# Queries and keys of a softmax attention block projected by Strassen's method

## Chip, cores, metric

One core of a Trainium2 chip. The metric is the device time of one execution in microseconds (us); of several runs the median is given.

## The reference, cut to what matters

Two attention blocks read the same x (2048 tokens, 1024 features, 32 heads of 32) and are mixed by a gate. Block A is a linear attention, block B a softmax attention. All inputs are float32.

```python
x = A_x                                             # 2048 x 1024
g = sigmoid((x * gate_w).sum(-1, keepdims=True))
a = A_ref(x, A_wqkv, A_wo)                          # linear attention
b = B_ref(x, B_wqkv, B_wo)
out = g * a + (1 - g) * b

def B_ref(x, wqkv, wo):                             # wqkv: 1024 x 3072
    q, k, v = heads(x @ wqkv)
    p = softmax(q @ k.T * 32 ** -0.5)
    return heads_joined(p @ v) @ wo
```

The change is in `x @ wqkv` of block B: the columns of queries and keys (the first 2048).

## The kernel before

**Products of three.** An operand of a projection is split into a rounded upper part (`copy` on ACT, called hi) and the remainder (`tensor_sub`, lo); `split` does both. `three` issues three matmuls for each 128 rows of the contraction: hi by hi, hi by lo, lo by hi. One matmul has a 128x128 stationary and a 128x512 moving operand. The contraction of 1024 is `NK` = 8 such steps, so a 128x512 output takes 24 matmuls.

**Stages, in order.**
1. *Value chunk 0 of block B* (512 of 1024 columns). x transposed (`xT`) is loaded in 128x512 pieces, split, and stays in `big[0]` to `big[15]` (128x2048 tiles). The first 8 token tiles go through all 8 steps of the contraction together, in 8 banks, as x arrives; the other 8 follow tile by tile.
2. *Queries and keys of block B.* `order` runs over 8 groups `g` of 128 columns, 4 token chunks `j` of 512, and `sec` (0 queries, 1 keys): 64 units. The weights' columns are stationary, x is moving; a unit's output (4 heads by 512 tokens) is split by ACT and DVE and both parts are stored to `qk_d`. Beside it run two generators, one step per unit: `gate` (loads 128x512 of x into one buffer, and multiplies it by `gate_w` with a running sum on DVE in its next step) and `spill` (stores both parts of x, two transfers a unit, to `xs`, for the later projections of block A).
3. *Value chunk 1*, as the first 16 units of the generator `linear`; its stationary operand is the x that is still in SBUF (`xstat`). `load_head(0)` comes at its fifth unit, `load_head(1)` at its sixth. The score maxima of head 0 (`maxima`) are mixed into these units.
4. *The rest*: the heads of block B (`heads_`), the linear projections of block A from the spilled x (`load_half`, three buffers `xh_t`), the output.

Up to stage 2 the instructions of every engine stand in program order. From stage 3 on a planner chooses at each step which of the generators issues next, by modelled times `T` of the engines; on the chip, too, every engine runs its instructions in the order written. All loads and stores are issued by SyncE (SP) in that order, and SP waits for what a transfer needs before it issues it.

**Names that the change touches.** `xpart` (a resident piece of x), `want_x`, `want_w`, `want_g` and `pump` (loads of stages 1 and 2 with six raw buffers), `v_out` (a value tile's way out), `gate`, `spill`, `load_half`, `linear`. `bank[0]` to `bank[7]` are the eight PSUM banks. Line 157, 160 and 162 of the profile are the matmuls of `three`, 300 and 301 the two halves of `split`, 427 the gate's multiplication, 176 every DMA on SP, 853 to 867 the fills in `load_q` and `load_k`.

## Time and profile before

| | us |
|---|---|
| median of 3 runs | 2867.18 (2864.64 to 2867.98) |
| span of the profiled execution, first to last instruction | 2865.2 |
| TensorE busy | 2856.9 |
| ScalarE (ACT), VectorE (DVE), GpSimd (POOL) busy | 1525.8, 2037.4, 1909.1 |

The page gives no own time for the profiled execution beside its span; the median of the runs is 2.0 us above that span. DVE, ACT and POOL are the engines of the element-wise work; PE is TensorE, PEld its weight loads. A row such as `L301 DVE TENSOR_TENSOR mid<-bank,mid 128x512 ... x64 | 44.2, 691` is line 301 of the kernel, 64 instructions that read a bank and `mid` and write `mid`, busy for 44.2 us together and 691 ns each. Rows of a timeline begin with the start and the duration in us; what stands in brackets is the idle time before it and what ended that. Rows of the windows begin with a stretch of the span; they give its length, the busy time and number of instructions of each engine, the granted TensorE clock, the share of the 16 DMA engines that was busy, and GB/s.

### The profile page before, as it was taken

Reading aid. Unit: us, or ns where it says so; the run is one execution under the profiler, and the core shown is the slowest. Engines: PE = TensorE matmul, PEld = TensorE weight load, DVE = VectorE, ACT = ScalarE, POOL = GpSimd, SP = SyncE. Lnnn points to the kernel's source line nnn. Section 1 sums busy time; section 2 is a strip of 40 time slices with the busy share of each in tenths; the row PEclk is TensorE's granted clock in tenths of the full one; section 3 lists DMA queues with packets and bytes.
Section 4 is the critical chain, followed back from the end, with each engine's and each line's share of the span. In section 5 each row is a group of like instructions: output and inputs, shape, how many; then the busy total and the mean of one; then the engine's idle time right before and its main releaser. Section 6 shows DMA issues by size and latency. Waiting matters only on the chain.

```text
span 2865.2 us, 46266 instructions
## 1 busy us (share of the span) xinstructions
PE 2856.9 (100%) x16136; PEld 2089.8 (73%) x16136; DVE 2037.4 (71%) x3372; ACT 1525.8 (53%) x2866; POOL 1909.1 (67%) x894
## 2 busy tenths in 40 slices
PE   9999999999999999999999999999999999999999
PEld 8888888867766776677767777777676666676787
DVE  3232113888888888888888888788888887887522
ACT  4111111466676667666666666566666665666400
POOL 0000001299999999999999999889889888885000
PEclk9999999999999999999999999999999999999999
DMA  6687333333343434333434344455656554634542
GB/s 198 209 268 243 121 121 107 108 90 98 101 133 98 104 100 129 93 96 95 128 106 100 100 119 139 143 171 171 201 173 190 135 161 138 160 109 132 195 151 77
DMA packets 348292, 394.97 MB, mean 138 GB/s; under 512 B 103214, under 2 KB 192558, under 8 KB 348060
## 3 DMA queue, kind: packets, MB, share of 16 engines
q1 hardware_dynamic: 334460, 378.91, 43.6%
q0 software_dynamic: 13600, 13.11, 3.4%
q8 instruction: 128, 2.10, 0.3%
q14 instruction: 104, 0.85, 0.1%
HBM read 268.70 MB, written 108.79 MB: 132 GB/s over the span
## 4 chain that ended last, share of the span: by engine, by line
PE 99%; DMA 1%; ACT 0%; issue 0%; SPq 0%; POOL 0%; DVE 0%; ACTq 0%
PE bank L1076 17%; PE bank L157 16%; PE bank L160 16%; PE bank L902 16%; PE bank L162 16%; PE bank L1233 16%; PE bank L967 1%; PE bank L686 1%; PE bank L575 0%; PE bank L959 0%; DMA big<-wa 0%; DMA big<-in_a_wqkv 0%; PE bank L646 0%; ACT big L1079 0%; PE bank L919 0%; DMA extra<-in_b_wqkv 0%
## 5 line engine op out<-in xcount | busy, mean ns | idle before, releaser
L1168 POOL TENSOR_TENSOR big<-big,big 128x512 f32<-128x512 f32 (+2 forms) x694 | 1643.5, 2372 | 119.1 <-ACT big L1079 76.5
L907 DVE TENSOR_REDUCE mx<-bank 128x1 f32<-128x512 f32 x2048 | 1308.2, 681 | 297.0 <-PE bank L902 292.9
L1079 ACT ACTIVATE big<-bank 128x512 f32<-128x512 f32 x2048 | 1179.8, 601 | 432.9 <-PE bank L1076 361.0
L1076 PE MATMUL bank<-big,big 128*128 128x512 f32 x1888 | 742.4, 394 | 0.2 <-ACT big L1079 0.2
L902 PE MATMUL bank<-big,big 128*128 128x512 f32 x1888 | 739.7, 392 | 0.3 <-ACT big L1079 0.3
L157 PE MATMUL bank<-big,big 128*128 128x512 f32 x1704 | 665.2, 390 | 0.4 <-ACT big L300 0.4
L160 PE MATMUL bank<-big,big 128*128 128x512 f32 x1704 | 664.0, 390 | 0.0
L162 PE MATMUL bank<-big,big 128*128 128x512 f32 x1700 | 662.5, 390 | 0.0
L1233 PE MATMUL bank<-big,mid 128*32 128x512 f32 x4096 | 454.1, 593 | 0.0
L1076 PEld LDWEIGHTS bank<-big,big 128*128 128x128 f32 x1888 | 354.1, 188 | 125.6 <-issue 46.9
L902 PEld LDWEIGHTS bank<-big,big 128*128 128x128 f32 x1888 | 354.5, 188 | 75.1 <-ACT big L1079 2.9
L157 PEld LDWEIGHTS bank<-big,big 128*128 128x128 f32 x1704 | 320.0, 188 | 69.7 <-issue 0.8
L160 PEld LDWEIGHTS bank<-big,big 128*128 128x128 f32 x1704 | 320.0, 188 | 67.0 <-DVE big L301 0.2
L162 PEld LDWEIGHTS bank<-big,big 128*128 128x128 f32 x1700 | 319.2, 188 | 66.3
L1233 PEld LDWEIGHTS bank<-big,mid 128*32 128x32 f32 x4096 | 142.7, 110 | 265.1 <-issue 265.1
L853 POOL MEMSET big<- 32x512 f32 (+1 forms) x4 | 3.7, 949 | 458.2 <-PE bank L160 458.2
L1184 DVE TENSOR_TENSOR bank<-bank,big 128x512 f32<-128x512 f32 x364 | 251.2, 690 | 5.9 <-ACT big L1079 3.9
L301 DVE TENSOR_TENSOR mid<-bank,mid 128x512 fp32r<-128x512 f32 x64 | 44.2, 691 | 263.4 <-ACT mid L300 263.4
L300 ACT CAST mid<-bank 128x512 fp32r<-128x512 f32 x64 | 37.6, 587 | 291.6 <-PE bank L162 272.2
L1164 POOL TENSOR_TENSOR big<-big,big 128x1536 f32<-128x1536 f32 (+1 forms) x31 | 121.4, 3915 | 40.3 <-ACT big L1079 40.3
L157 PE MATMUL bank<-big,xh 128*128 128x512 f32 x344 | 135.2, 393 | 1.7 <-ACT big L1079 1.1
L160 PE MATMUL bank<-big,xh 128*128 128x512 f32 x344 | 134.8, 392 | 0.3 <-DMA big<-wa 0.3
(95 smaller groups left out, 1735.8 us busy)
## 6 DMA issues: line engine op xcount, KB each, us to landing
big<-xs SPq DMA_DIRECT2D x256, 256.0 KB
big<-qk SPq DMA_DIRECT2D x720, 64.0 KB
qk<-mid SPq DMA_DIRECT2D x128, 256.0 KB
xh<-xs SPq DMA_DIRECT2D x128, 256.0 KB
big<-oA SPq DMA_DIRECT2D x84, 256.0 KB
xs<-big SPq DMA_DIRECT2D x64, 256.0 KB
oA<-mid SPq DMA_DIRECT2D x64, 256.0 KB
big<-big POOLq DMA_DIRECT2D x50, 256.0 KB, 5.6
```

Source lines behind the costliest of these rows:

```text
L157: yield nc.tensor.matmul(ps, sh, mh_, start=(kt == 0), stop=False)
L160: yield nc.tensor.matmul(ps, sh, ml_, start=False, stop=(late and kt == NK - 1))
L162: yield nc.tensor.matmul(ps, sl, mh_, start=False, stop=(kt == NK - 1))
L301: eng.tensor_sub(lo, src, f32(hi))
L902: nc.tensor.matmul(bank[b], q[:, t % TPC * P:(t % TPC + 1) * P], k[:, j * C:(j + 1) * C], start=True, stop=True)
L907: nc.vector.tensor_reduce(m[:, t, j:j + 1], bank[b], AX.X, ALU.max)
L1076: nc.tensor.matmul(bank[b], k[:, t * P:(t + 1) * P], q_cols(h, j), start=True, stop=True)
L1079: nc.scalar.activation(pr_t[i][:, j * C:(j + 1) * C], bank[b], AF.Exp, scale=SCALE)
L1164: nc.gpsimd.tensor_add(lacc[:, :qp], pr(0)[:, :qp], pr(1)[:, :qp])
L1168: nc.gpsimd.tensor_add(lacc[:, sl], lacc[:, sl], pr(t)[:, sl])
L1184: nc.vector.tensor_add(lacc[:, qp:] if t == NT - 1 else l_b[:, :n], l_b[:, :n], src)
L1233: nc.tensor.matmul(av_b[j * DH:(j + 1) * DH, :], v[:, t, :], pr(t)[:, j * C:(j + 1) * C], start=(t == 0), stop=(t == NT - 1))
```

## The change

The tokens are taken in two halves `J` of 1024, the contraction as 4 pairs of steps (even `l = 0`, odd `l = 1`), and two column groups `g`, `g+1` of queries or keys are computed at a time by Strassen's method in Winograd's form: a *quad* has four outputs of 128x512 (two groups by two token chunks) from seven products of 4 steps (`KH`), 12 matmuls each.

- **Sides of x.** From the four raw pieces of a pair POOL makes T1 to T4 (`sides`), which ACT and POOL split (`split_sides`, `last_side`). X11, T1, T2, X21, T3, X22 and T4 are the moving operands of products 0 to 6. T4 takes the place of X12 once X12 was used by the value pass and spilled.
- **Weights.** Four 128x512 raw tiles per quad (`load_quad`, two quads ahead) are combined by DVE and split by ACT with DVE or POOL (`quad_weights`, during the quad before) into a ring of 14 slots. They are loaded and made once for each half of the tokens.
- **Sums.** `quad` issues the products into six banks in turn; DVE adds them up in `P1`, `U2`, `W2`, `C22`. Each output is split by ACT and POOL and stored in two transfers.
- **Beside a quad**, one step of each after every product: the next quad's weights, T4 (in the first quad of a half), a spill of x, and a step of the gate. The gate now takes 128x256 pieces (64 steps) in one buffer, `gate_x`. The eighth quad of a half has other company: `change` or `leave`.
- **Value chunk 0** is computed in each half before its quads (`v_pass`, 8 tiles at once). Its split weights are stored in the first half (`store_wv`) and loaded again for the second (`load_wv_again`).
- **Value chunk 1** no longer finds x in SBUF: `linear` takes it from `xs` by `load_half`, as the projections of block A do. `load_head(0)` comes at its first unit, `load_head(1)` at its second.

The core of the diff:

```diff
+    def sides(raws, i):
+        r11, r12, r21, r22 = raws
+        nc.gpsimd.tensor_sub(r11, r12, r11)
+        nc.gpsimd.tensor_sub(r12, r22, r12)
+        nc.gpsimd.tensor_sub(r22, r22, r11)
+        nc.gpsimd.tensor_sub(t4_raw[i], r21, r22)
...
+    def quad_weights(raws, J, f):
+        w11, w12, w21, w22 = raws
...
+        part(0, w11, nc.gpsimd)
+        part(6, w22, nc.vector)
+        nc.vector.tensor_add(w22, w21, w22)
+        nc.vector.tensor_sub(w21, w11, w21)
+        yield
+        part(1, w22, nc.gpsimd)
+        nc.vector.tensor_sub(w11, w22, w11)
+        yield
+        part(3, w12, nc.gpsimd)
+        part(2, w11, nc.vector)
+        yield
+        nc.vector.tensor_sub(w12, w12, w11)
+        part(4, w21, nc.gpsimd)
+        yield
+        part(5, w12, nc.vector)
+
+    def quad(J, f, side):
+        sec, g = quad_cols(f)
+        def product(s):
+            ps = bank[next(turns) % NQB]
+            n = quad_ring(J, f, s)
+            for i in range(KH):
+                sl = slice(i * P, (i + 1) * P)
+                stat = [ring_w(n, p)[:, sl] for p in range(2)]
+                for _ in three(ps, stat, [xpiece(J, PRODUCTS[s], p, i) for p in range(2)], i, n=KH):
+                    pass
+            return ps
+        def store(i, jj, src, hi):
+            split(f32r(hi), f32r(src), src, nc.gpsimd)
+            j = 2 * J + jj
+            for p, part in enumerate((hi, src)):
+                dma(qk_d[sec][p][g + i][:, j * C:(j + 1) * C], part)
+        nc.scalar.copy(P1, product(0))
+        next(side, None)
+        p5 = product(1)
+        next(side, None)
+        nc.vector.tensor_add(U2, product(2), P1)
+        nc.vector.tensor_add(W2, p5, U2)
+        next(side, None)
+        nc.vector.tensor_add(P1, product(3), P1)
+        store(0, 0, P1, H11)
+        next(side, None)
+        p7 = product(4)
+        nc.vector.tensor_add(C22, p7, W2)
+        nc.vector.tensor_add(U2, p7, U2)
+        store(1, 1, C22, H22)
+        next(side, None)
+        nc.vector.tensor_add(W2, product(5), W2)
+        store(0, 1, W2, H12)
+        next(side, None)
+        nc.vector.tensor_add(U2, product(6), U2)
+        store(1, 0, U2, H21)
+        next(side, None)
...
+    def gate():
+        dma(zrep, bass.AP(tensor=gate_w.tensor, offset=gate_w.offset, ap=[[0, P], [1, D]]))
+        for t in range(NT):
+            for i in range(NG):
+                dma(gate_x, x[t * P:(t + 1) * P, i * GW:(i + 1) * GW])
+                yield
+                nc.vector.scalar_tensor_tensor(bank[7][:, :GW], gate_x, 1.0, zrep[:, i * GW:(i + 1) * GW],
+                                               op0=ALU.mult, op1=ALU.mult, accum_out=tg[:, t * NG + i:t * NG + i + 1])
...
+    def quads(J, first, spills):
+        sides_ = [late_side(J), spills, gates]
+        for f in range(QUADS - 1):
+            if f + 2 < QUADS:
+                load_quad(raws_q[f % 2], f + 2)
+            else:
+                first()
+            quad(J, f, beside(quad_weights(raws_q[(f + 1) % 2], J, f + 1), *sides_))
...
     def linear():
...
-            if n == (TPC if kind == "v" else 0):
+            if n == 0:
                 load_head(0)
                 load_v(0)
-            if n == (TPC + 1 if kind == "v" else 0):
+            if n == 1:
                 load_head(1)
                 load_v(1)
             for k in range(NK):
...
-                stat = xstat(t, k) if kind == "v" else [xstat_lin(n, k, p) for p in range(2)]
+                stat = [xstat_lin(n, k, p) for p in range(2)]
...
-                if kind != "v" and k % HK == HK - 1:
+                if k % HK == HK - 1:
                     load_half(2 * n + k // HK + 3)
```

394 lines of the change are left out of this document (255 added, 139 removed).

## Prediction

> **What bounds the kernel now.** I read the page first (span, engines, chain), then TensorE's waits.
>
> ```profile
> span 2865.2 us, 46266 instructions
> PE 2856.9 (100%) x16136; PEld 2089.8 (73%) x16136; DVE 2037.4 (71%) x3372; ACT 1525.8 (53%) x2866; POOL 1909.1 (67%) x894
> PE 99%; DMA 1%; ACT 0%; issue 0%; SPq 0%; POOL 0%; DVE 0%; ACTq 0%
> PE bank L157 <- ACT big L300: 0.4, 1, 0.4
> ```
>
> TensorE is busy for the whole span, carries 99% of the chain that ended last, and its one wait near the projections is 0.4 us. A matmul taken out therefore shortens the span by its full spacing, and a wait put in lengthens it by its full length. Next, the stages (window; PE, PEld, DVE, ACT, POOL busy; clock; DMA share; GB/s): queries and keys, value chunk 1 behind them, and two parts of the first.
>
> ```profile
> 92.30:440.60 348.30, 348.30 (x1539) 288.45 (x1538) 84.06 (x164) 54.89 (x98) 0.00 (x0) 1.00 0.62 195
> 440.60:548.00 107.40, 107.40 (x476) 88.84 (x475) 60.51 (x90) 17.23 (x31) 11.38 (x9) 1.00 0.38 114
> 100.00:250.00 150.00, 150.00 (x664) 124.23 (x663) 43.76 (x95) 22.58 (x40) 0.00 (x0) 1.00 0.86 267
> 300.00:440.00 140.00, 140.00 (x619) 115.94 (x618) 26.34 (x40) 22.30 (x40) 0.00 (x0) 1.00 0.36 121
> 446.68 0.39 PE L160 MATMUL bank<-big,big 128*128 128x512 f32 x1
> 457.56 0.39 PE L160 MATMUL bank<-big,big 128*128 128x512 f32 x1
> ```
>
> The stage has 1536 matmuls by its loops (64 units of 24); the row counts 1539 with its edges. The two single rows are 48 matmuls apart, so one costs 10.88/48 = 0.2267 us, and 1536 of them 348.2 us, the stage. In it DVE, ACT and POOL are mostly idle, but while x is spilled and the gate read (100 to 250 us) the DMA engines are at 0.86 and 267 GB/s, which makes 267/0.86 = 310 GB/s, or 0.85 us for a 256 KB transfer alone.
>
> **Part 1, matmuls removed.** A quad makes four 128x512 outputs in 7 products of 12 matmuls: 84 for 96. Two halves of 8 quads are 1344, 192 fewer: 192 x 0.2267 = **43.5 us** off the path. Value matmuls are as many as before. A quad lasts 84 x 0.2267 = 19.04 us, a product 2.72.
>
> **Part 2, the arithmetic added beside them.** Durations of the same tile sizes (line, engine, operation; count, busy us, mean ns):
>
> ```profile
> L300 ACT CAST big<-mid 128x512 fp32r<-128x512 f32 x81 | 50.2, 632 | 13.7 <-DMA mid<-in_xT 8.7 <-DMA mid<-in_b_wo 4.0 <-DMA mid<-in_b_wqkv 0.3
> L301 DVE TENSOR_TENSOR mid<-bank,mid 128x512 fp32r<-128x512 f32 x64 | 44.2, 691 | 263.4 <-ACT mid L300 263.4
> L510 POOL TENSOR_TENSOR big<-mid,big 128x512 fp32r<-128x512 f32 x14 | 18.0, 1296 | 2.7 <-ACT big L508 2.7
> L427 DVE SCALAR_TENSOR_TENSOR big<-big,zrep 128x512 f32<-128x512 f32 x32 | 21.9, 684 | 2.3 <-DMA big<-in_x 2.1
> L427 DVE DVE_READ_ACCUMULATOR big<-big,zrep 128x1 f32 x32 | 2.6, 82 | 0.0
> ```
>
> Per quad DVE gets 7 sums of products, 4 of weights and 3 splits (14 x 0.69 = 9.7 us), POOL 8 subtractions (10.4), ACT 12 copies (7.6). Each fits under 19.04, so as throughput this costs nothing; the cover is the quad's own matmuls and six banks, which let DVE trail TensorE by five products, 13.6 us. What trails further is paid in full.
>
> **Part 3, the gate, one chunk per product.** Before, a gate step (load 256 KB of x, multiply) came once per unit of 24 matmuls, 5.44 us, with one buffer. After, it comes once per product, 2.72 us, again with one buffer (gate_x, 128 KB): 64 steps, 49 in the first half's quads and 15 in the second's. DVE, in order, waits in each step for the load issued in the step before, and SP may issue the next load only after that multiply. So a step lasts at least load time + multiply. Queued behind the waiting DVE are the sums that free the banks and the weights of the next quad.
>
> How long is the load? The nearest rows:
>
> ```profile
> 0.76 0.39 SPq L176 DMA_DIRECT2D mid<-in_xT  x1
> 2.77 0.30 ACT L300 CAST big<-mid 128x128 fp32r<-128x128 f32 x1 [0.74 <-DMA mid<-in_xT]
> ...
> 133.68 0.33 SPq L176 DMA_DIRECT2D big<-in_x  x1
> 134.05 0.98 SPq L176 DMA_DIRECT2D xs<-big  x2
> 138.77 0.69 DVE L427 SCALAR_TENSOR_TENSOR big<-big,zrep 128x512 f32<-128x512 f32 x1 [0.89 <-DMA big<-in_x]
> 253.80 0.52 SPq L176 DMA_DIRECT2D big<-in_x  x1
> 257.92 0.69 DVE L427 SCALAR_TENSOR_TENSOR big<-big,zrep 128x512 f32<-128x512 f32 x1 [0.36 <-DMA big<-in_x]
> ```
>
> 64 KB with nothing ahead took 2.0 us; the gate's 256 KB among stores and spills 4.1 and 5.1. For 128 KB with nothing ahead I take 2.2 (the first row plus 0.2 for the added 64 KB at 310 GB/s). The multiply of 256 columns: half of 684 ns plus 82, 0.45.
> - Step without store or spill: 2.2 + 0.45 = 2.7 us, just the product's time.
> - Steps 3 to 6 also store an output, and the gate load stands behind that on SP: sum 0.69, copy 0.63, subtraction 1.30, issue of the lower part 0.35: 3.0 us. Then the load runs half behind that store (2.2 + 0.4) and is multiplied (0.45). DVE starts the next sum after the previous step's multiply, so two steps overlap: about 6.3 us for two, 3.1 each.
> - At each quad's start four weight loads go ahead (4 x 0.85 = 3.4 of transfer, part of it over before the gate's issue): 3 us once.
> - A spill ahead (24 of them, one per step from quad 0 on, 0.85 of transfer, less its own issue) adds 0.5.
>
> A quad without spills: 3 x 2.7 + 4 x 3.1 + 3 = 23.5 us; with spills 3.5 more, 27. First half: 3.43 quads with and 3.57 without are 176.5 us, against 49 x 2.72 = 133.3: 43 behind. The cover takes 13.6, and 8 is already counted at the entry (Part 4): **22 us**. Second half: 15 steps with spills, 2.14 x 27 = 58 against 41: 17, less 13.6 of cover: **3 us**. Bounds: with 2.0 us in every step nothing is behind (0); with 4.1 in the 39 steps that spill, 39 x (4.55 - 2.72) + 25 x 0.64 (23.5/7 less 2.72) - 27 = 60.
>
> **Part 4, entries.** POOL makes the sides of x: 28 subtractions per half, 36.4 us, under a value pass of 192 x 0.2267 = 43.5. In the first half x starts it at about 10 us, so the last raw tiles come free near 49, quad 1's weights land near 54, and the gate's first multiply needs zrep (512 KB) behind eight value stores: DVE is 8 to 10 us behind when it makes T4, which product 6 needs. I take **8 us** (bounds 0 and 14). In the second half POOL shares four raw buffers with two more loads of 1 MB (about 5 us each, 4 x 0.85 + 2) and starts some 5 late, behind a tile whose store queues after sixteen loads of split weights: 36.4 + 10 + 5 against 43.5, **8 us** for quad 0 and as much again, **8**, for its T4, which waits for X12's spill; within the pass the x of k = 4 to 7 comes **6 us** late. Bounds for these 22: 3 and 35.
>
> **Part 5, value chunk 1 from DRAM.** Before, x was resident there. After, each unit loads 1 MB in halves, three ahead (8.2 us of matmuls), and head 0 is loaded in unit 0, head 1 in unit 1, both ahead of the next halves on SP:
>
> ```profile
> 464.04 8.37 SPq L176 DMA_DIRECT2D big<-qk  x18
> 472.46 0.65 SPq L176 DMA_DIRECT2D mid<-v  x1
> 474.51 8.40 SPq L176 DMA_DIRECT2D big<-qk  x18
> 482.95 1.57 SPq L176 DMA_DIRECT2D mid<-v  x1
> ```
>
> SP is at head 0 some 3 us into the stage (the last quad's store), issues for 9.0, then half 3: lands near 15 where 8.2 was due, 7 us. Head 1 holds SP for 10 us again: half 5 lands near 27, TensorE is through with half 4 near 20.5: 6.5. Up to seven score matmuls fill 1.6. **12 us** (bounds 8 and 17). Later units need 1.25 MB per 5.44 us, 230 GB/s, under the 310.
>
> **Sum.** -43.5 + 22 + 3 + 8 + 22 + 12 = +23.5. On the profiled execution that is 2865.2 + 23.5 = 2888.7 of span; the median of the runs (2867.18) is 2.0 above the span, for what lies around it, so **2891 us**.
>
> **A rule weighed.** After the last matmuls the profile shows the clock:
>
> ```profile
> 2860.00:2863.00 3.00, 1.10 (x5) 0.56 (x3) 0.75 (x1) 0.00 (x0) 0.00 (x0) 1.00 0.08 29
> 2863.00:2866.00 3.00, 0.00 (x0) 0.00 (x0) 0.00 (x0) 0.00 (x0) 0.00 (x0) 0.52 0.16 58
> ```
>
> Idle from 2861.1, it is at half about 2 us later. So a pause of 2 us or more may leave the next matmuls at half speed for a while; no row shows for how long, since no pause of that kind occurs before the end. The Trainium skill (TensorE: Matmul & The Clock Gate, Part 1) says that an idle window of about 3.4 us halves the clock and a busy one restores it; the row agrees on the fall. By that page a restart costs an estimated 1.7 us, and the sum would be some 8 us more for the pauses outside the gate's loop (inside it DVE sets the pace).
>
> **Rivals.**
> - Faster: the gate loads land in time. Decided at 2.72 - 0.45 = 2.27 us per load: below it DVE never trails beyond its cover, and T4 and the second entry shrink with it to about 5 in all. For it: 2.0 us for an unhindered load. Against: stores, spills and weights on the same queue, and 4.1 to 5.1 in the stage of before. Time: -43.5 + 12 + 5 = -26.5, 2841 us.
> - Transfers are the bound while x is spilled: a quad moves 5.9 MB there (2.1 stores, 1.8 spills, 1.0 weights, 0.9 gate), in 19.04 us 310 GB/s, just the limit above. Loads at 4.1 us: 60 for the gate in place of 25: +58.5, 2926. Against: the loop slows its own demand.
> - Clock: each of some 15 pauses (seven quads, entries, two in the units) is followed by as much at half speed as it takes to fall, 2 us, so 1 us lost each: 15 us more, 2906. No pause in the profile shows it.
> - Balance: landings of 2.5 to 2.6 us cost 40 to 47: 2863 to 2871.
>
> **How the numbers follow.** Forecast with its spread (bounds of Parts 3 to 5) 0.52; clock 0.08; faster rival 0.25; transfers as the bound, or worse, 0.08; balance 0.07. Differences within 0.2% (5.7 us), about what a measurement of this kernel can tell, are most of the balance: 0.06. Faster 0.27, with the balance's low edge; slower 0.67. The range goes from the faster rival, 2841, to the transfer bound, 2926; beyond it I leave half of what lies past either end.
>
> **What would show it.** Right: 1344 product matmuls at 0.2267; TensorE's waits in the first half's quads, on banks and weights that DVE and POOL were late with, DVE's own waits naming gate_x's load; quads of 23 to 27 us where the gate runs and 19.04 where it has ended; two pauses of some 7 us in units 1 and 2 of the value chunk. Wrong: quads of 19 us in the first half (Part 3 falls, about 2845), or no pauses in the value units.

## The result and the profile after

The changed kernel takes 2949.27 us (median of 4, 2949.03 to 2953.04) against 2866.77 (2864.64 to 2867.98): 1.029 times the time of before, 95% interval 1.0276 to 1.0305. Forecast were 2891, range 2841 to 2926: the sign was right, the loss three and a half times what was forecast (82 us against 24), and the time lies above the range.

The page of the changed kernel (span, engines, the chain that ended last), and beside it its waits (engine and tile, what was waited for: us in all, times, longest):

```profile
span 2947.3 us, 46931 instructions
PE 2848.4 (97%) x15944; PEld 2070.4 (70%) x15944; DVE 2204.3 (75%) x3568; ACT 1598.0 (54%) x2994; POOL 2170.3 (74%) x1082
PE 85%; DMA 4%; issue 1%; POOL 1%; DVE 1%; ACT 0%; SPq 0%; DVEq 0%; POOLq 0%; ACTq 0%
DVE bank L497 <- DMA kvb<-in_x: 100.4, 56, 3.9
PE bank L152 <- DVE mid L469: 32.7, 8, 7.2
```

192 matmuls are gone (16136 before, 15944 now). They should have taken 43.5 us of TensorE's busy time with them, but that fell by only 8.5 (2856.9 to 2848.4). Most of the 35 us between them are matmuls at half clock: in the stretches where the granted clock is 0.50, TensorE is busy for 56.9 us, half of which is lost. A further 90.6 us (82.1 of span and 8.5 of busy time) are pauses that TensorE did not have before. Its share of the chain falls from 99% to 85%; that of DMA rises from 1% to 4%. DVE waits 100.4 us for the gate's loads (line 497 multiplies the piece in `kvb`, the buffer of `gate_x`), 56 times. TensorE waits 32.7 us for line 469, the sum that frees the bank of product 1.

The stages in windows (stretch; PE, PEld, DVE, ACT, POOL busy; clock; DMA share; GB/s): quads 0 and 2 of the first half, quad 4 of the second, where gate and spills have ended, the two value passes, and the start of value chunk 1:

```profile
62.10:90.30 28.20, 22.44 (x85) 17.52 (x86) 13.60 (x21) 11.53 (x21) 10.45 (x8) 0.86 0.63 206
111.90:138.40 26.50, 19.32 (x84) 15.68 (x84) 14.28 (x29) 6.81 (x12) 10.53 (x8) 0.90 0.73 222
422.40:441.40 19.00, 19.00 (x85) 15.76 (x84) 11.62 (x14) 6.92 (x12) 11.20 (x9) 1.00 0.56 181
4.70:62.10 57.40, 44.89 (x193) 36.69 (x192) 45.08 (x31) 23.99 (x44) 49.74 (x32) 0.94 0.76 244
265.30:325.80 60.50, 46.62 (x193) 37.25 (x193) 25.93 (x21) 19.57 (x36) 48.21 (x35) 0.89 0.60 195
498.60:540.00 41.40, 25.60 (x94) 19.46 (x93) 6.25 (x9) 2.75 (x5) 13.25 (x10) 0.84 0.73 204
```

The third row is the change as it was meant: 84 matmuls in 19.0 us, the clock whole, no pause. All of the second half's quads 4 to 7 are like it. The gate's quads last 21.7 to 28.1 us, the value passes 57.4 and 60.5 in place of 43.5. Measuring each stage from its first matmul to the next stage's first, less its matmuls at 0.2267 us, gives the ledger:

| stage | lost, us | forecast |
|---|---|---|
| first value pass | 13.9 | with quads 0 to 6: 22 + 8 |
| first half, quads 0 to 6 | 9.1, 2.6, 7.5, 7.9, 6.3, 6.2, 5.5: 45.1 | |
| first half, quad 7; second value pass; second half, quad 0 | 5.8, 16.9, 5.8: 28.5 | 22 |
| second half, quads 1 to 3 (gate's last steps, spills) | 3.5, 8.3, 2.9: 14.7 | 3 |
| from value chunk 1 on (the remainder) | 23.4 | 12 |
| all | 125.6 | 67 |

125.6 - 43.5 = 82.1. Where a pause of TensorE has a length below, it is counted from the start of the last matmul before it to the start of the next, so it is some 0.4 us above the idle time in the rows.

**The gate's loop**, in the first half's quad 2 (start, duration, engine, line; in brackets the idle time before and what ended it):

```profile
120.75 0.69 DVE L479 TENSOR_TENSOR mid<-bank,mid 128x512 f32<-128x512 f32 x1
120.91 0.33 SPq L169 DMA_DIRECT2D kvb<-in_x  x1
...
123.86 0.43 DVE L497 SCALAR_TENSOR_TENSOR bank<-kvb,zrep 128x256 f32<-128x256 f32 x1 [2.43 <-DMA kvb<-in_x]
124.22 0.69 DVE L482 TENSOR_TENSOR mid<-bank,mid 128x512 f32<-128x512 f32 x1
124.51 0.60 SPq L169 DMA_DIRECT2D kvb<-in_x  x1
```

The multiply frees the buffer, SP issues the next load some 0.2 us behind it, and 2.95 us after the issue of 120.91 the next multiply starts. Behind it stands the sum (line 482) that frees a bank. From issue to issue it is 3.60 us, where a product takes 2.72.

**How far DVE trails.** The gate's first multiply; the sum of product 1 in quad 6, and quad 7's first matmul, which takes the bank that this sum frees; the first half's last multiply:

```profile
79.02 0.43 DVE L497 SCALAR_TENSOR_TENSOR bank<-kvb,zrep 128x256 f32<-128x256 f32 x1 [3.63 <-DMA kvb<-in_x]
...
239.64 0.69 DVE L469 TENSOR_TENSOR mid<-bank,mid 128x512 f32<-128x512 f32 x1
240.48 0.47 PE L152 MATMUL bank<-big,big 128*128 128x512 f32 x1 [2.36 <-DVE mid L469]
...
255.56 0.43 DVE L497 SCALAR_TENSOR_TENSOR bank<-kvb,zrep 128x256 f32<-128x256 f32 x1 [2.76 <-DMA kvb<-in_x]
```

In a loop on time the first multiply would stand two products into quad 0, at 62.1 + 5.4 = 67.6. It comes 11.5 us later: its load stands on SP behind eight value stores, four loads of weights, a spill and `zrep`. The 47 turns from there to 255.56 take 3.76 us each, 49 us more than 47 products, so DVE ends 60 us behind. TensorE may run ahead of it by five products, 13.6 us, and does: quad 7 starts when DVE has just added up product 1 of quad 6. That sum ends 58.5 us later than product 1 would have ended without any wait (62.1 + 6 x 19.04 + 2 x 2.72 = 181.8), and 58.5 - 13.6 = 44.9 is what TensorE had lost by then (45.1).

**The entry.** POOL and DVE slow each other when both read SBUF. The clearest rows come later, in the second half's quad 4, where there is little else; behind them one POOL operation of the first pass, at 32.69, and the group of DVE's splits in the first 49 us:

```profile
422.39 1.29 POOL L294 TENSOR_TENSOR mid<-mid,mid 128x512 fp32r<-128x512 f32 x1 [0.22 <-ACT mid L293]
422.60 0.69 DVE L482 TENSOR_TENSOR mid<-bank,mid 128x512 f32<-128x512 f32 x1 [0.99 <-PE bank L157]
...
426.60 1.28 POOL L294 TENSOR_TENSOR big<-mid,big 128x512 fp32r<-128x512 f32 x1 [1.24 <-ACT big L293]
427.02 1.41 DVE L294 TENSOR_TENSOR big<-mid,big 128x512 fp32r<-128x512 f32 x1 [3.73 <-ACT big L293]
428.46 0.69 DVE L428 TENSOR_TENSOR mid<-mid,mid 128x512 f32<-128x512 f32 x1
...
32.69 1.73 POOL L373 TENSOR_TENSOR big<-big 128x512 f32<-128x512 f32 x1
```
```profile
L294 DVE TENSOR_TENSOR big<-big,big 128x512 fp32r<-128x512 f32 x16 | 24.3, 1574 | 3.6 <-ACT big L293 3.6
```

With one operand in a bank DVE takes its 0.69 us within POOL's operation (422.60). With both in SBUF (427.02) it ends 0.55 after POOL's end at 427.88, 1.41 us in all, and alone, at 428.46, it takes 0.69 again. In the first value pass, where both have one such operation after another, DVE's takes 1.57 on average and POOL's 1.6 to 1.75 in place of 1.29. The Trainium skill (SBUF — State Buffer; SBUF: two separate sides) says that a DVE operation with two SBUF inputs and a GpSimd operation that reads SBUF share a port pair by an exclusive lock, and the later waits for the whole of the earlier. The trace agrees that it waits, and that an operand in PSUM spares it; strict turns would give 1.98 us a pair (0.69 + 1.29). Measured were 1.6 to 1.8 for each of the two, side by side, and that is what counts here.

So POOL's 32 operations in the first value pass take 49.7 us (41.3 at 1.29 each), and quad 0's weights come late. ACT stands in program order behind them, the value tiles' copies (line 356) behind those, and TensorE waits for their banks:

```profile
60.97 0.62 ACT L293 CAST big<-extra 128x512 fp32r<-128x512 f32 x1 [5.86 <-DVE extra L437]
61.49 2.04 ACT L356 COPY mid<-bank 128x512 f32<-128x512 f32 x4
62.12 0.79 PE L152 MATMUL bank<-big,big 128*128 128x512 f32 x1 [12.54 <-ACT mid L356]
```

**Value chunk 1.** SP's issues, and TensorE's waits there:

```profile
492.02 11.36 SPq L169 DMA_DIRECT2D qk<-mid  x8
503.47 8.33 SPq L169 DMA_DIRECT2D big<-qk  x18
...
512.54 2.68 SPq L169 DMA_DIRECT2D big<-xs  x4
...
515.75 10.98 SPq L169 DMA_DIRECT2D big<-qk  x18
...
510.49 1.86 PE L1126 MATMUL bank<-big,big 128*128 128x512 f32 x7 [3.61 <-DMA big<-qk]
518.58 0.80 PE L152 MATMUL bank<-big,big 128*128 128x512 f32 x1 [6.23 <-DMA big<-xs]
531.71 0.80 PE L152 MATMUL bank<-big,xh 128*128 128x512 f32 x1 [5.62 <-DMA xh<-xs]
```

The halves of x (`xs`) wait on SP behind the last quad's stores and each head's 18 loads, as forecast: the second and third of the pauses (6.6 and 6.0 us). The first (4.0 us) was not forecast: score matmuls of head 0 wait for their own load (`qk`), where the prediction had them fill time.

**The clock** around the pause before quad 3 (same columns as the stages above):

```profile
131.40:138.40 7.00, 0.00 (x0) 0.00 (x0) 4.13 (x8) 0.62 (x1) 1.90 (x2) 0.64 0.85 235
138.40:143.50 5.10, 5.05 (x12) 4.06 (x13) 3.18 (x9) 1.14 (x2) 2.17 (x2) 0.50 0.47 150
143.50:146.00 2.50, 2.50 (x12) 2.06 (x12) 1.84 (x2) 1.14 (x2) 1.83 (x2) 0.99 0.81 255
```

The clock falls within the pause and stays at half for 5.1 us after it: 12 matmuls there, 12 in the next 2.5 us.

### The profile page after: what moved, and what is told of

It is laid out like the page before. It is cut to its first block, busy times and chain, and to the rows that moved or that the text cites. A ratio compares the mean times of both kernels' runs of the same rounds, so it can differ in the third digit from the quotient of the medians.

```text
span 2947.3 us, 46931 instructions
## 1 busy us (share of the span) xinstructions
PE 2848.4 (97%) x15944; PEld 2070.4 (70%) x15944; DVE 2204.3 (75%) x3568; ACT 1598.0 (54%) x2994; POOL 2170.3 (74%) x1082
## 4 chain that ended last, share of the span: by engine, by line
PE 85%; DMA 4%; issue 1%; POOL 1%; DVE 1%; ACT 0%; SPq 0%; DVEq 0%; POOLq 0%; ACTq 0%
PE bank L1300 16%; PE bank L1126 16%; PE bank L1457 15%; PE bank L152 12%; PE bank L155 12%; PE bank L157 12%; DMA kvb<-in_x 2%; PE bank L1191 1%; PE bank L907 1%; DMA big<-wa 0%; PE bank L796 0%; DMA big<-wv 0%; SPq L169 0%; POOL big L294 0%; DMA big<-xs 0%
## 5 line engine op out<-in xcount | busy, mean ns | idle before, releaser
L1126 PE MATMUL bank<-big,big 128*128 128x512 f32 x1888 | 738.7, 392 | 4.8 <-DMA big<-qk 3.6
L1300 PE MATMUL bank<-big,big 128*128 128x512 f32 x1888 | 742.3, 394 | 0.5 <-ACT mid L356 0.5
L152 PE MATMUL bank<-big,big 128*128 128x512 f32 x1600 | 637.0, 398 | 73.7 <-DVE mid L469 32.7
L155 PE MATMUL bank<-big,big 128*128 128x512 f32 x1600 | 633.8, 396 | 6.4 <-POOL big L294 5.4
L157 PE MATMUL bank<-big,big 128*128 128x512 f32 x1596 | 631.0, 395 | 0.4 <-DVE big L294 0.4
L1300 PEld LDWEIGHTS bank<-big,big 128*128 128x128 f32 x1888 | 353.9, 188 | 126.8 <-issue 48.6
L1126 PEld LDWEIGHTS bank<-big,big 128*128 128x128 f32 x1888 | 354.3, 188 | 80.6 <-ACT big L1303 4.2
L152 PEld LDWEIGHTS bank<-big,big 128*128 128x128 f32 x1600 | 306.8, 192 | 146.7 <-issue 36.7
L155 PEld LDWEIGHTS bank<-big,big 128*128 128x128 f32 x1600 | 307.0, 192 | 72.2 <-POOL big L294 6.0
L157 PEld LDWEIGHTS bank<-big,big 128*128 128x128 f32 x1596 | 305.4, 191 | 65.7 <-DVE big L294 0.8
L294 POOL TENSOR_TENSOR mid<-mid,mid 128x512 fp32r<-128x512 f32 x64 | 83.4, 1304 | 164.6 <-ACT mid L293 164.5
L152 PE MATMUL bank<-big,xh 128*128 128x512 f32 x384 | 151.6, 395 | 6.4 <-DMA xh<-xs 5.6
L155 PE MATMUL bank<-big,xh 128*128 128x512 f32 x384 | 151.0, 393 | 0.7 <-DMA big<-wa 0.7
L157 PE MATMUL bank<-big,xh 128*128 128x512 f32 x384 | 150.6, 392 | 0.3 <-DMA xh<-xs 0.3
L293 ACT CAST mid<-mid 128x512 fp32r<-128x512 f32 x64 | 39.7, 621 | 180.1 <-issue 68.7
## 6 DMA issues: line engine op xcount, KB each, us to landing
big<-xs SPq DMA_DIRECT2D x300, 256.0 KB
xh<-xs SPq DMA_DIRECT2D x148, 256.0 KB
qk<-mid SPq DMA_DIRECT2D x128, 256.0 KB
big<-oA SPq DMA_DIRECT2D x84, 256.0 KB
xs<-big SPq DMA_DIRECT2D x64, 256.0 KB
oA<-mid SPq DMA_DIRECT2D x64, 256.0 KB
big<-big POOLq DMA_DIRECT2D x50, 256.0 KB, 5.6
```

Of the source, the lines that this page charges most:

```text
L152: yield nc.tensor.matmul(ps, sh, mh_, start=(kt == 0), stop=False)
L155: yield nc.tensor.matmul(ps, sh, ml_, start=False, stop=(late and last))
L157: yield nc.tensor.matmul(ps, sl, mh_, start=False, stop=last)
L294: eng.tensor_sub(lo, src, f32(hi))
L1126: nc.tensor.matmul(bank[b], q[:, t % TPC * P:(t % TPC + 1) * P], k[:, j * C:(j + 1) * C], start=True, stop=True)
L1300: nc.tensor.matmul(bank[b], k[:, t * P:(t + 1) * P], q_cols(h, j), start=True, stop=True)
```

## The experiments

Ratios are to the kernel before, timed on the same chip, with their 95% intervals. Line numbers are each kernel's own. "Lost" is the ledger's measure.

**1. The gate's loads and multiplications left out.**

```diff
-                dma(gate_x, x[t * P:(t + 1) * P, i * GW:(i + 1) * GW])
-                yield
-                nc.vector.scalar_tensor_tensor(bank[7][:, :GW], gate_x, ...
...
+        nc.vector.memset(tg, 0.0)
...
```

> Leaves out the gate's loads of x and its multiplications (the gate's sum is taken as zero); all else as in the changed kernel. Theory (the one-buffer gate loop sets the pace of the quads that it runs beside): quads 0.2 to 0.6, 24.5 to 27.0 us now, come to 19.0 to 20, and so does quad 1.2 (27.4); some 55 us less in all, about 2895 us. Rival (spills, stores and weights fill the DMA queues, or the element-wise engines are too slow): the quads that spill stay above 24 us, under 15 us less in all, above 2934.

2883.14 us, 1.0058 (1.0041 to 1.0074): 66 us less than the change. First the change, then this kernel, 62 to 265 us:

```profile
62.00:265.00 203.00, 167.81 (x672) 134.76 (x672) 110.94 (x206) 57.96 (x105) 78.65 (x60) 0.90 0.62 194
```
```profile
62.00:265.00 203.00, 198.93 (x864) 163.52 (x864) 110.91 (x129) 73.87 (x131) 123.52 (x91) 0.99 0.64 205
```

192 matmuls more in the same time, at a whole clock and about the same DMA share. The first half's quads 1 to 7 and the second's 1 to 7 all last 19.0 us. What is left ahead of value chunk 1 (13.6 in the first value pass, 5.5 in quad 0, 11.9 in the second pass, 2.3 behind it) belongs to the entries. Quad 7, the second pass and quad 0 of the second half lose 14.2 together, where they lost 28.5. The gate is by far the largest cause.

**2. Heads 0 and 1 loaded in units 4 and 5 of value chunk 1** in place of 0 and 1.

```diff
-            if n == 0:
+            if n == TPC:
                 load_head(0)
-            if n == 1:
+            if n == TPC + 1:
                 load_head(1)
```

> Heads 0 and 1 are loaded at the fifth and sixth unit of value chunk 1, as in the kernel before, not at the first and second. Theory (the 38 head transfers ahead of the next halves of x on SP make the pauses in units 1 and 2): the pauses of 4.0, 6.6 and 6.0 us near 506 to 532 go, and with them the half clock after them, about 20 us less, 2929 us; a smaller pause may come at the fifth unit. Rival (the units cannot stream 1 MB of x each): the pauses only move, under 5 us less.

2946.93, 1.0276 (1.0261 to 1.0292): 2.3 less. The pauses of 2.2, 5.6 and 5.5 us come at 527 to 549 us instead. The expectation fell: on SP's queue the pauses only moved.

**3. The value tiles copied out ahead of the last weights and sides**, in both halves.

```diff
+    for t in range(2 * TPC):
+        v_out(0, t, bank[V_BANKS[0][t]], v_outs[t % 4])
     split_sides(raw_x0[3], 0, 3)
     load_quad(raw_b, 1)
     for _ in quad_w:
         pass
-    for t in range(2 * TPC):
-        v_out(0, t, bank[V_BANKS[0][t]], v_outs[t % 4])
...
```

> At the end of each value pass ACT copies the eight value banks out before the last weight and side copies of the first quad, not after them. Theory (the first product waits for a bank whose copy stands behind weight copies on ACT): the pauses of 12.9 us (first half) and 13.8 us (second) shrink to 3 to 5 us; part of that comes back as a longer wait for T1 or T4 in the first quad; 10 to 18 us less, 2931 to 2939. Rival (POOL's and DVE's chain of sides and weights is late whatever ACT does): the wait moves by the same length to the first products, under 4 us less.

2948.72, 1.0284 (1.0268 to 1.0299): the pause of 12.9 us is gone (1.0 lost in the first pass), but quad 0 loses 15.6 in place of 9.1, and the second half's quad 0 15.7 in place of 5.8. Of the first pass and quad 0 together 6.4 of 23.0 us go, of the second pair 4.2 are added. ACT's order mostly chose which wait is seen; DVE and POOL were late either way.

**4. Twenty idle matmuls ahead of product 0**, in the first half's quads 2 to 6 and the second's 0 to 2, to hold the clock.

```diff
+        if 2 <= f + 8 * J <= 10 and f < 7:
+            for _ in range(20):
+                nc.tensor.matmul(bank[6][:, :P], ones, ones, start=True, stop=True)
         nc.scalar.copy(P1, product(0))
```

> Adds 20 matmuls of 128x128 float32 on an idle bank, about 4.5 us, ahead of the first product of quads 0.2 to 0.6, 1.0 to 1.2, where TensorE waits anyway, so that it does not fall idle and keeps its full clock. Theory (inside the gate's loop DVE sets the pace, the half clock is hidden): those quads keep their length, the time is within 5 us of 2949. Rival (the half clock after each pause, 6.8 to 13.7 us long in ten places, costs half of that each): some 15 to 25 us less.

2954.65, 1.0302 (1.0287 to 1.0318): 5 more.

```profile
62.00:265.00 203.00, 184.30 (x872) 153.63 (x872) 109.88 (x204) 56.79 (x101) 77.97 (x59) 0.94 0.62 190
```

The clock rises from 0.90 to 0.94 and nothing is won: the first half's quads 2 to 6 lose 32.5 us in place of 33.4. In the second half the idle matmuls put off quad 0 by 7 us, and quads 1 to 3 lose 7 less. Inside the loop half-clock matmuls only fill time in which TensorE would wait for DVE.

**5. Two buffers for the gate.** Pieces go in turn to `kvb` and to two 128x128 tiles, and a piece is multiplied two steps after its load was issued.

```diff
+                if len(left) == 2:
+                    gate_mul()
+                c = t * NG + i
+                parts = [(gate_x, i * GW, GW, tg[:, c:c + 1])]
+                if i % 2:
...
+                    parts = [(f32(mh_full), i * GW, GH, ...), (f32(ml_full), i * GW + GH, GH, ...)]
+                for buf, at, n, acc in parts:
+                    dma(buf, x[t * P:(t + 1) * P, at:at + n])
+                left.append(parts)
...
```

> The gate gets a second buffer (two tiles of 128x128 that are idle in this stage) and multiplies what was loaded two steps before; loads and multiplications are the same in size, with 32 chunks taken in two parts. Theory (a step lasts load plus multiply because of the one buffer): a load now has two products' time, 5.4 us, where 2.3 to 4.0 are needed, so quads 0.1 to 0.6 and 1.1 to 1.2 come to 19 to 20 us: 45 to 65 us less, 2885 to 2905. Rival (the added element-wise work of the gate or its DMA traffic as such is too much beside a quad, so that only leaving it out helps): quads with spills stay above 24 us, less than 20 us gained.

2912.99, 1.0159 (1.0142 to 1.0176): 36 less, under the expected 45 to 65.

```profile
62.00:265.00 203.00, 188.80 (x786) 152.65 (x787) 140.95 (x260) 66.93 (x120) 104.64 (x77) 0.96 0.74 228
DVE bank L500 <- DMA kvb<-in_x: 19.0, 12, 3.9
DVE bank L500 <- DMA mh<-in_x: 15.1, 10, 4.6
```

DVE's waits for the gate fall from 100.4 us to some 34, and the first half's quads 1 to 6 lose 0 to 4.4 each. Even a load issued two steps ahead is at times not there.

**6. The 28 subtractions per half moved from POOL to DVE** (16 that make the sides, 12 of their splits).

```diff
-        nc.gpsimd.tensor_sub(r11, r12, r11)
+        nc.vector.tensor_sub(r11, r12, r11)
...
-            split(xpiece(J, name, 0, i), xpiece(J, name, 1, i), raw, nc.gpsimd)
+            split(xpiece(J, name, 0, i), xpiece(J, name, 1, i), raw, nc.vector)
```

> All subtractions and splits of T1 to T3 and the raw T4 (28 per half) go from POOL to DVE. Theory (DVE operations with both inputs in SBUF and POOL operations slow each other down when they run at once: 1.6 to 1.8 us for 0.69 on DVE, 1.6 for 1.29 on POOL in the value pass): alone on DVE the pass's 52 operations of 0.69 us are 36 us, under the pass of 43.5; the excess of the first value pass and quad 0.0, 23 us, falls to 6 to 12, that of the second, 22.7, by about as much: 15 to 30 us less, 2920 to 2934. Rival (two engines in parallel are needed, the slow operations are no fault of each other): DVE with 52 operations of up to 1.7 us is late, and the time is above 2949.

2933.90, 1.0230 (1.0215 to 1.0246): 15 less. The change and this kernel, 5 to 62 us:

```profile
5.00:62.00 57.00, 44.59 (x192) 36.40 (x191) 44.67 (x31) 23.62 (x44) 49.74 (x32) 0.94 0.76 245
```
```profile
5.00:62.00 57.00, 56.18 (x243) 46.11 (x244) 43.73 (x62) 29.14 (x54) 7.34 (x5) 1.00 0.90 292
```

This carries the point on contention: DVE does 62 instructions in 43.73 us where it did 31 in 44.67, and 27 of POOL's 32 are gone. The first pass loses 2.0 in place of 13.9. The same edit also takes work off POOL, so the gain is not contention alone. Quads 0 to 6 still lose 47.9 (45.1 in the change): the gate's loop starts as late as there, with its first multiply 17 us into quad 0 (at 67.5, quad 0 at 50.4; 79.0 and 62.1 in the change).

**7. Heads 0 and 1 loaded during the last quad.**

```diff
         for k in range(KH, NK):
+            if k - KH < 2:
+                load_head(k - KH)
             split_v1(raw_b[k - KH], k)
             yield
...
             if n == 0:
-                load_head(0)
                 load_v(0)
             if n == 1:
-                load_head(1)
                 load_v(1)
...
```

> Heads 0 and 1 are loaded in the third and fourth step of the last quad, where SP is idle, ahead of the value units; only their value tiles stay in units 0 and 1. Theory (38 head transfers hold SP for 20 us, wherever in the units they stand; moving them to the fifth unit moved the pauses there): the three pauses of 16.6 us in units 1 to 3 and 13.7 us of half clock go: 17 to 23 us less, 2926 to 2932. Rival (1 MB of x per unit is too much for the queue in itself): pauses stay, under 5 us less.

2946.30, 1.0276 (1.0261 to 1.0292): 3 less, far from the expected 17 to 23.

```profile
492.63 11.09 SPq L169 DMA_DIRECT2D big<-qk  x18
504.75 8.85 SPq L169 DMA_DIRECT2D big<-qk  x18
513.70 3.31 SPq L169 DMA_DIRECT2D qk<-mid  x6
525.02 0.79 PE L152 MATMUL bank<-big,big 128*128 128x512 f32 x1 [14.84 <-DMA big<-xs]
```

Three pauses became one of 15 us: now the last quad's stores and the halves of x stand behind 36 loads.

**8. Edits 5, 6 and 7 in one.**

> The second gate buffer, the sides on DVE and the heads in the last quad together. If the three causes are separate, their gains add up: some 55 + 22 + 20 = 97 us less than 2949, about 2852, which is 15 us under the kernel before; with 43.5 us of matmuls saved, some 28 us of waits would be left. If they share one cause (a busy DMA queue), the sum is less than the largest two together: above 2875.

2891.08, 1.0082 (1.0067 to 1.0097): 58 less than the change; the three alone gave 36 + 15 + 3 = 54, so they add up, but not to the forecast. Left: 12.3 in the second value pass, 2 to 6 in many quads, and one pause of 13 us in value chunk 1.

**9. Heads 0 and 1 on POOL's DMA queue**, at the place of the change.

```diff
+        put = nc.gpsimd.dma_start if h < 2 else dma
...
         for b, p in enumerate((0, 0, 1)):
-            dma(f32(q[b * DH:(b + 1) * DH, :]), qk_d[0]...
+            put(f32(q[b * DH:(b + 1) * DH, :]), qk_d[0]...
...
```

> The 36 loads of heads 0 and 1 (queries and keys) are issued on POOL's queue in place of SP's, at the same place in the program; the halves of x stay on SP. If the three pauses of value chunk 1 come from SP's time for issuing these loads (about 0.5 us each, the halves of x behind them), they go with it, with the half clock behind them: 2949 - 17 to 20 = 2929 to 2932. Rival (the transfers themselves, or the DMA engines' time, delay the halves of x): the pauses stay within a third of what they were, 2944 to 2949.

2942.25, 1.0265 (1.0248 to 1.0282): 7 less; forecast were 17 to 20 or under 5. The pauses over 1 us at 506 to 520 us sum to 8.2 in place of 16.6. SP's issue time is at most about half of the pauses: POOL issues these loads between its other work, from 503 to 536 us, so that they are spread as well, and this run does not part the two.

**10. The split value weights loaded four at a time** over the steps of the first half's last quad.

```diff
-        load_wv_again(range(NK - 1))
+        load_wv_again((0, 1))
...
+        load_wv_again((2, 3))
...
```

> The sixteen loads of split value weights in the first half's last quad are issued four at a time over the quad's steps, in place of fourteen at once at its start. If the second half's value pass loses its 16.9 us because stores of the last quad queue behind those loads on SP (so that a raw tile of T4 cannot be overwritten, and DVE waits), about 11 of it go: 2949 - 8 to 11 = 2938 to 2941. Rival (the pass waits for POOL's sides of x whatever the order of the loads): at most 3 less, 2946 to 2949.

2949.65, 1.0287 (1.0271 to 1.0302): nothing. The pass lost 12.9 in place of 16.9, quads 6 and 7 before it 2.5 more. In the second pass ACT, and TensorE behind it, wait for weights that are loaded late, after their raw tiles came free:

```profile
309.38 0.62 ACT L293 CAST big<-mid 128x512 fp32r<-128x512 f32 x1 [4.38 <-DMA mid<-in_b_wqkv]
```

**11. Edits 5, 6, 9 and 10 in one.**

> Four edits in one: two buffers for the gate, sides of x on DVE, heads 0 and 1 on POOL's queue, value weights loaded four at a time. The version of before with the first two and the heads in the last quad took 2891.1. If the two theories on SP's queue hold, 16 us of the pause in value chunk 1 and 8 to 11 of the second value pass go from it: 2864 to 2868, level with the kernel before. Rival (they fall): 2880 to 2891.

2885.07, 1.0062 (1.0046 to 1.0077): inside the rival's range, 6 us under experiment 8. The two theories on SP's queue brought little of what they promised. Value chunk 1 still has three pauses of 1.5 to 3.2 us.

**12. Edit 9, with the heads' loads spread over units 4 to 10 (counted from 0).**

```diff
+            if n in (TPC, 2 * TPC):
+                h = n // TPC - 1
+                load_q(h, 0)
+                load_q(h, 1, NJ)
+                load_v(h)
+            if n in (TPC + 2, 2 * TPC + 2):
+                for j in range(NJ):
+                    load_k(n // TPC - 1, j)
```

> As the version with heads 0 and 1 on POOL's queue (2942.3), but later and spread: queries of head 0 in the fifth unit of value chunk 1, its keys in the seventh, head 1 in the ninth and eleventh, when the halves of x are three ahead again. If what is left of the pauses there (16 us of the 23 lost) comes from the heads' transfers landing just when SP has been held by the last quad's stores, most of it goes: 2928 to 2932. If the heads' transfers delay the halves of x wherever they stand, the pauses move to units five to eleven and the time stays at 2938 to 2943. If it is the last quad's stores alone, a pause of 3 to 6 us stays at units one and two: 2932 to 2936.

2938.57, 1.0257 (1.0240 to 1.0275): 4 less than edit 9, and most of the pauses moved with the loads, to 530 to 539 us: the second case, at its lower end.

```profile
510.00:520.00 10.00, 8.83 (x37) 6.64 (x38) 0.00 (x0) 0.81 (x2) 7.31 (x12) 1.00 1.04 302
530.00:540.00 10.00, 5.19 (x20) 2.99 (x18) 0.00 (x0) 0.59 (x1) 5.69 (x12) 0.99 1.08 257
```

The DMA engines are busy throughout (the share goes above 1, so it is not exact) at 257 to 302 GB/s. With SP out of the way, this points to the transfers as the bound wherever the heads are loaded; no run takes them away, so it is not shown.

**13. The gate at half the rate in the first half**: a step per two products there (24 of 64), one per product in the second half (39).

```diff
+        def slow():
+            while True:
+                next(gates, None)
+                yield
+                if J == 0:
+                    yield
-        sides_ = [late_side(J), spills, gates]
+        sides_ = [late_side(J), spills, slow()]
```

> The gate is stepped once per two products in the first half's quads (24 steps in place of 49, as rare as in the version of before), and once per product in the second half's (39 in place of 15, to quad 5). One buffer, as in the change. If the gate's step, about 3.4 us, is late only since it comes every 2.72 us, the first half's quads 1 to 7 lose most of their 42 us of excess (left: 0 to 10), and the second half's quads 0 to 5 go from 20 to 34 to 40: 2949 - 15 to 22 = 2927 to 2934. Rival (the sums are late for the weights, spills and stores, and the gate only adds transfers): first half's quads keep 25 or more, and the total is 2949 or above.

2927.43, 1.0211 (1.0196 to 1.0226): 22 less, in the expected 15 to 22.

```profile
62.00:265.00 203.00, 196.16 (x846) 160.73 (x846) 127.55 (x171) 71.53 (x127) 119.67 (x86) 0.98 0.69 216
```

The first half's quads 1 to 6 all last 19.0 us, one buffer or not, with the spills, stores and weights of the change beside them. So one buffer is enough at this rate: the step fits 5.44 us, as before the change, and not 2.72. More bytes move here than in the change (216 GB/s, 194 there), so spills, stores and weights are not what made the sums late. The second half pays 19 us for the steps that it takes over (1.5, 7.9, 8.8, 5.6, 6.4 and 2.4 in quads 1 to 6).

**14. Edits 5, 6, 10, 12 and 13 in one**, and the last quad's stores on POOL's queue.

```diff
+            put = nc.gpsimd.dma_start if (J, f) == (1, QUADS - 1) else dma
             for p, part in enumerate((hi, src)):
-                dma(qk_d[sec][p][g + i][:, j * C:(j + 1) * C], part)
+                put(qk_d[sec][p][g + i][:, j * C:(j + 1) * C], part)
```

> All edits that helped, in one: two buffers for the gate, the slow gate in the first half, sides of x on DVE, value weights four at a time, heads 0 and 1 on POOL's queue and late, the last quad's stores on POOL's queue too. Taken from 2885.1 (four of these in one): value chunk 1 loses 10 to 13, the first half's quads 12 to 17, and the second half's gain 3 to 8: 2856 to 2870, so about level with before or faster. Rival (the gains overlap, since the same DVE and DMA time is freed by each): 2872 to 2885.

2865.85, 0.9999 (0.9989 to 1.0008): level with before, inside the expected range. Quads 2 to 7 of the first half last 19.0, the value passes lose 2.0 each.

**15. Edit 12, with the heads' value columns in units 12 and 14.**

```diff
-                load_v(h)
...
+            if n in (3 * TPC, 3 * TPC + 2):
+                load_v((n - 3 * TPC) // 2)
```

> As the version with the heads on POOL's queue and late (2938.6), but the value columns of heads 0 and 1 (256 KB each, read in rows of 128 bytes) are loaded in units 13 and 15 in place of 5 and 9. There the pause of 3.5 us and 3.4 us at half clock follow the first of those loads. If its many small packets delay the halves of x, they go, and nothing new comes where no head is loaded: 2933 to 2936. Rival (the heads' queries and keys fill the DMA engines, and the pause is theirs): within 2 of 2938.6.

2941.47, 1.0261 (1.0245 to 1.0278): 2.9 more than edit 12, outside both ranges but on the rival's side. The pause of 3.5 us at 536 went, and one of 2.6 came at 607 in place of 1.2. So the value columns' small packets are not the matter in the total.

**16. Edit 14 changed in three things**: the gate steps twice per three products in both halves, the heads' loads are thinned to 192 to 576 KB per unit over units 2 to 10 (counted from 0) with the value columns in 12 and 14, and the last quad's stores are back on SP.

```diff
+                for _ in range(2):
+                    next(gates, None)
+                    yield
+                yield
...
+        HEADS.update({2 + 5 * h: [(load_q, h, 0), (load_k, h, 0)], 3 + 5 * h: [(load_k, h, 1), (load_k, h, 2)],
+                      4 + 5 * h: [(load_k, h, 3)], 5 + 5 * h: [(load_q, h, 1, NJ)], 12 + 2 * h: [(lambda h: load_v(h), h)]})
```

> The version with all edits (2865.9), changed in three things: the gate is stepped twice per three products in both halves, the loads of heads 0 and 1 are thinned to 192 to 576 KB per unit over units 3 to 11 with the value columns in units 13 and 15, and the last quad's stores are back on SP's queue. That version still loses about 18 us in value chunk 1 and 7.5 in the second half's quads 3 to 6. If transfers bound value chunk 1 wherever they are bunched, 8 to 13 of the first go, and 3 to 6 of the second: 2847 to 2856, faster than before by 0.4 to 0.7%. Rival (the chunk has no room for the heads at any rate): 2858 to 2863.

2857.41 (median of 5), 0.9964 (0.9950 to 0.9979): faster than before by 0.36%, between the forecast and its rival.

```profile
span 2857.5 us, 47070 instructions
PE 2828.5 (99%) x15944; PEld 2056.2 (72%) x15944; DVE 2251.9 (79%) x3690; ACT 1597.9 (56%) x2994; POOL 2109.6 (74%) x1062
62.00:265.00 203.00, 195.99 (x847) 160.73 (x846) 160.06 (x252) 77.82 (x137) 91.35 (x66) 0.98 0.80 246
```

TensorE's busy time falls by 28.4 of the 43.5 us. All quads but the first two of the first half and the first of the second last 19.0 to 19.5 us. It is 8.4 us under edit 14 by the medians, 3.8 in the profiled executions (2861.3 to 2857.5), there all from the quads. Left are 16 us in the entries and quads and about 20 from value chunk 1 on, where edit 14 lost about 17: thinner loads did not make room there, as the rival said. Pauses and half clock of some 9 us lie in the chunk's first three units; where the other 11 go is not settled.

## Why the prediction was right or wrong

- **Matmuls removed, -43.5: right.** A quad without company lasts 19.0 us, and with the gate left out nearly all do.
- **Gate, first half, 22 with 8 for the entry: the step that failed is "8 is already counted at the entry".** The 43 us by which the sum has DVE fall behind count from a loop that starts on time. The late start, which Part 4 itself put at 8 to 10 us (11.5 measured), comes on top of them; the sum took it out of them. The turns were longer as well, 3.76 us in place of 176.5/49 = 3.60, which is 7 us in 47 turns. So DVE ended 60 us behind, not 43, and TensorE lost 45.1 in quads 0 to 6 where 30 were forecast. The cover of 13.6 was real: all of it was given. But it is given once, and the late start spends it too: DVE adds up quad 0's last product 6.3 us after quad 1 has started, quad 1's 12.3 us after quad 2 has, and stays at 11.5 to 12.4 from there on. Quad 1 loses 2.6, quads 2 and 3, with the cover gone, 7.5 and 7.9.
- **A figure that was right by luck.** TensorE's quads 0 to 6 took 178.4 us, near the sum's 176.5, but the sum is of DVE's loop, and that took 193.9 (62.1 to 256.0). The length of one quad was forecast well: 27 us with spills (26.5 and 27.0 measured in quads 2 and 3), 23.5 without (24.5 to 25.4).
- **Entry, first half, 8 (0 to 14): a term was missing.** Quad 0's wait for T4 was foreseen; quad 0 lost 9.1, and 5.5 even with no gate. Not foreseen was a pause of 12.9 before quad 0, with POOL and DVE slowing each other (49.7 us for POOL's 32 operations in place of 41.3); experiment 6 takes the pause away. "Each fits under 19.04, so as throughput this costs nothing" and "36.4 us, under a value pass" took durations measured alone.
- **Gate, second half, 3: the same step; 14.7.** The first multiply comes 7 us late (335.8; one product into quad 0 is 328.5), and 15 turns take 4.10 us each, where the sum had 58/15 = 3.87. At product 1 of quad 2 DVE is 31.0 us behind; less 13.6 this is 17.4, and TensorE had lost 17.6 in quads 0 to 2. Quad 3 loses 2.9 more, at half clock.
- **Second entry, 22: 28.5**, inside its bounds of 3 and 35, in part by luck, for the mechanism was partly another: raw tiles free late and their weights landing late, and 5.8 for the first reload of the split value weights, which no term had. Half of it hangs on the gate: without it 14.2 are left (experiment 1).
- **Value chunk 1, 12: 23.4, over its upper bound of 17.** SP's issue time was the right mechanism for at most about half of the pauses, 7 of the 23.4 us (experiment 9). The prediction took the transfers to be free because 230 GB/s lay under 310; with a head's loads added the engines are full (experiment 12). A third pause, of score matmuls that wait for head 0's own load, and the half clock behind the pauses came on top.
- **Clock.** As a rival it gave 15 us. Inside the loop it costs nothing (experiment 4). Outside it, matmuls run at half clock at the starts of quad 0, both ends of the second value pass and behind the second and third pauses of chunk 1, for about 21 us, so 10.5 are lost. The 8 us that the prediction estimated from the window of the Trainium skill (TensorE: Matmul & The Clock Gate, Part 1) was near, and should have gone into the sum. By the trace's record of the granted clock the stretches at half last 3.4, 6.8, 10.2 or 13.7 us, whole multiples of that page's window of about 3.4; apart from quad 0's three short pauses, the clock fell 2.4 to 5.6 us after a pause began.
- **Rivals.** "The gate loads land in time" fell: 2.95 us from issue to multiplication in the rows above, where it needed 2.27. "Transfers the bound while x is spilled" was wrong in the first half's quads (experiment 13's quad 1 moves 274 GB/s, spills among them, from 86 to 105 us, and lasts 19.0). Experiment 12 points to it in value chunk 1, where it was not placed.

Sum of the misses: 15.1 in the first half's quads 0 to 6 (45.1 less 30), 13.9 in the first value pass, 11.7 in the second half's quads 1 to 3, 6.5 at the second entry, 11.4 in chunk 1: 58.6 us, the distance from +23.5 to +82.1.

## What to carry to other kernels

A saving on TensorE is worth what its companions can keep up with: a loop of load, multiply, load through one buffer that fitted a 5.44 us unit was late in every 2.72 us product, and slowing it again took 40 of the 45 us lost in the first half's quads 0 to 6 (and cost 19 in the second half, which took over its steps). Slack such as "six banks, five products" is given once. Add up all by which the engine behind will be late, its late start included, and take the slack off that sum; the lap of a loop alone does not tell where it starts. Durations measured alone were too short where DVE and POOL both read SBUF. And moving loads within one queue only moved the pauses that they made (experiments 2 and 7); another queue took 7 of 23 us.

## What the runs showed of the hardware

- DVE 128x512 with two SBUF operands beside POOL: 1.4 to 1.8 us in place of 0.69; POOL 1.6 to 1.75 in place of 1.29 where DVE is as busy. So 28 subtractions moved onto DVE cost DVE nothing (44.67 us for 31 instructions, 43.73 for 62).
- In the change the half clock comes in stretches of 3.4, 6.8, 10.2 and 13.7 us and outlasts a pause by up to 6.1 us (216.0 to 222.0).
- Moving 36 loads of 64 and 192 KB from SP's queue to POOL's was worth 7 us of the 23.4 lost from value chunk 1 on (experiment 9). Loads moved later, thinner or with the value columns apart gave at most 4 more; that the DMA engines' own time is the rest was not shown.
